# Transposing q and k by the DMA crossbar in place of TensorE, from the third batch on

## The chip, the cores and the metric

The kernel runs on one core of one Trainium2 chip. The metric is the device time of one execution in microseconds. Times are quoted as medians of several runs. A run counts as slow when it lies over 1.5% above the fastest of its kernel. Small differences can still be clear of noise, so 95% intervals are given.

## The reference, cut to what matters

A windowed attention with eight global tokens is followed by a two-layer network with a snake activation. Everything is bf16 inside the kernel.

```python
B, H, S, D = 8, 8, 576, 64              # q, k, v: float32 [B, H, S, D]
mask = (abs(i - j) <= 32) | is_global[i] | is_global[j]
attn = softmax(where(mask, q @ k.T / sqrt(D), -1e9))
x = (attn @ v).transpose(0, 2, 1, 3).reshape(B * S, H * D)      # [4608, 512]
h = x @ w_in                                                    # w_in [512, 2048]
g = h + sin(alpha * h) ** 2 / (alpha + 1e-9)
out = g @ w_out                                                 # w_out [2048, 512]
```

## The kernel before

The work goes in nine rounds. Round p has an attention stage for batch p (the ninth has none), whose gaps are filled with the second-layer matmuls of chunk p-1 (a chunk is 512 tokens), and then a first-layer stage for chunk p (16 blocks of four matmuls). q and k of batch p+1 are loaded in round p's attention stage, and the first two of its four head pairs are transposed inside round p's first-layer stage.

This kernel's scores matmul reads q and k with the head dimension on partitions, so both are transposed. TensorE does it through PSUM, six transposes for k and six for q of each head pair. VectorE spreads k into twelve overlapping key blocks, and ScalarE copies q.

```python
def stage_T(b, hp, qpool, qtag):
    QS, KS = qk[b]                                   # [96, 6, 8 heads, 64]
    for jt in range(NTW):                            # 6
        nc.tensor.transpose(out=Kps[:, WIN + jt * TW : WIN + (jt + 1) * TW],
                            in_=KS[:, jt, 2 * hp : 2 * hp + 2, :], ...)
    nc.vector.tensor_copy(out=kTw[hp][:, :, 0:KB], in_=...)       # from PSUM, 12 windows of 112
    Qps = qpool.tile([P, S], BF, name=qtag)
    for jt in range(NTW):
        nc.tensor.transpose(out=Qps[...], in_=QS[:, jt, 2 * hp : 2 * hp + 2, :], ...)
    nc.scalar.copy(out=qT[hp][:, :, 0:QB], in_=Qps[...])
# ... cut ...
def mm1(c, H2b, psB, sq):                            # first layer, 16 blocks
    for nt in range(NT):
        # four matmuls into one of six PSUM tiles h2
        # ScalarE: Sb = sin(alpha * h2)
        # S2 = Sb * Sb: ScalarE for block 5, VectorE for 10 and 15, POOL for the others
        # VectorE, two blocks later: H2b = S2 / alpha + h2   (frees h2)
# ... cut ...
# in the first-layer stage of round p, batch p+1:
i_ = (10, 13)
m1[i_[0]] = partial(chain, m1[i_[0]], partial(shift_v, p + 1), partial(global_v, p + 1),
                    partial(stage_T, p + 1, 0, psB, "hb"))
m1[i_[1]] = partial(chain, m1[i_[1]], partial(stage_T, p + 1, 1, psB, "hb"))
```

`shift_v` and `global_v` are three transfers on SyncE's queue. They prepare the v of batch p+1. The output stores are on that queue too. In all the timelines below, what the program put on SyncE's queue starts in the order of the program.

The softmax here doesn't subtract the row's maximum and nothing guards it: scores larger than these inputs give would overflow.

## Time and profile before

| | before |
|---|---|
| time, median | 385.99 us (385.66 to 386.37) |
| span of the profiled run | 385.0 us |
| five periods, first-layer stage of round 2 to that of round 7 | 38.5, 38.3, 38.0, 38.4, 38.0 us |

A period is the time from the first first-layer matmul of one round to that of the next. In the profile PE is TensorE and PEld its weight loads, DVE is VectorE, ACT ScalarE, POOL GpSimd and SP SyncE; a q behind a name is that engine's queue of instructions. The granted clock is the share of its full speed at which TensorE was allowed to run. First, from the page of the kernel before, the busy time of each engine, and the engines' shares of the chain of work that ended last:

```profile
PE 336.2 (87%) x3208; PEld 162.9 (42%) x3208; DVE 244.9 (64%) x551; ACT 258.4 (67%) x435; POOL 249.3 (65%) x394
...
PE 52%; ACT 18%; DVE 10%; issue 7%; POOL 7%; DMA 3%; POOLq 1%; ACTq 0%; DVEq 0%
```

Then two periods of it, by windows. The columns are the stretch, its length, busy time and count of PE, PEld, DVE, ACT and POOL, the granted clock, the share of the DMA engines, and GB/s.

```profile
167.28:205.63 38.35, 37.21 (x385) 18.04 (x384) 27.13 (x59) 29.59 (x50) 31.19 (x48) 1.00 0.93 97
205.63:243.60 37.97, 37.15 (x385) 18.05 (x384) 26.63 (x59) 29.58 (x50) 31.28 (x48) 1.00 0.94 98
```

TensorE is busy for nearly the whole period at full clock. The timeline of TensorE in one first-layer stage shows what the transposes take (start, duration, line, operation, tiles, shape, count, and in brackets the idle time before it and what ended it):

```profile
205.63 9.66 PE L457 MATMUL hb<-xT,w_in 128*128 128x512 bf16 x44
215.13 0.42 PE L304 MATMUL Kps<-identb,KS 96*128 96x96 bf16 x6
215.39 0.42 PE L319 MATMUL hb<-identb,QS 96*128 96x96 bf16 x6
215.64 2.76 PE L457 MATMUL hb<-xT,w_in 128*128 128x512 bf16 x12
218.87 0.42 PE L304 MATMUL Kps<-identb,KS 96*128 96x96 bf16 x6 [0.47 <-DVE kTw L310]
...
221.25 1.89 PE L494 MATMUL ops<-w_out,H2b 128*128 128x512 bf16 x8
```

The starts are 0.26 us apart, so six transposes take TensorE 0.26 us, and the eight groups of a batch take 2.1 us. The same stretch on VectorE:

```profile
216.11 1.28 DVE L472 TENSOR_TENSOR S<-Sb 128x512 bf16<-128x512 bf16 x1 [0.22 <-ACT Sb L464]
217.31 0.73 DVE L447 SCALAR_TENSOR_TENSOR H2b<-S,recipT,hb 128x512 bf16<-128x512 bf16 x1
217.97 0.84 DVE L310 COPY kTw<-Kps 128x1344 bf16<-128x1344 bf16 x1
218.74 2.05 DVE L447 SCALAR_TENSOR_TENSOR H2b<-S,recipT,hb 128x512 bf16<-128x512 bf16 x3
...
222.22 0.44 DVE L472 TENSOR_TENSOR S<-Sb 128x512 bf16<-128x512 bf16 x1
```

The same square takes 1.28 us while POOL squares beside it and 0.44 us after. In these 6.5 us VectorE works without a pause. SyncE's queue in this stage:

```profile
206.55 0.33 SPq L506 DMA_DIRECT2D out_dram<-osb  x1
207.18 0.51 SPq L121 DMA_DIRECT2D VW<-VW  x1
207.74 0.58 SPq L122 DMA_DIRECT2D VW<-VW  x1
208.37 0.78 SPq L127 DMA_DIRECT2D VW<-VgN  x1
```

### The profile page before, as it was taken

To read this page: it belongs to the slowest core of one execution; us is meant where nothing else is said; L and a number is where in the kernel's file an instruction comes from. 1 tells how busy PE (TensorE), PEld (TensorE's weight loads), DVE (VectorE), ACT (ScalarE), POOL (GpSimd) and SP (SyncE) were. 2 spreads that over 40 slices of the span, in tenths; PEclk is the share of its full clock that TensorE was granted. 3 is DMA by queue.
4 is the path that set the end of the run, shared out by engine and by line. 5 is a ranking of instruction groups with operands and counts; after the bars stand their busy time and mean duration, and the time that the engine had idled before them with its cause. 6 is when DMAs were issued, how large, how long until landed. Compare 5 with 4: busy or idle time off the path is not lost.

```text
span 385.0 us, 8609 instructions
## 1 busy us (share of the span) xinstructions
PE 336.2 (87%) x3208; PEld 162.9 (42%) x3208; DVE 244.9 (64%) x551; ACT 258.4 (67%) x435; POOL 249.3 (65%) x394
## 2 busy tenths in 40 slices
PE   1128499798999999999999999999999999999796
PEld 0015244443444444444544444444444444344342
DVE  7725459574977497649774976497749774954500
ACT  1057487786988588858885888578857885744310
POOL 8934396227878589858986898689768006854400
PEclk9999999999999999999999999999999999999989
DMA  6999999257999409940994099409940001000012
GB/s 53 136 162 161 190 164 165 37 77 77 155 132 153 124 9 103 148 127 7 103 148 126 7 103 149 128 6 113 137 128 5 30 30 54 2 28 27 29 54 82
DMA packets 133723, 35.31 MB, mean 92 GB/s; under 512 B 123314, under 2 KB 128178, under 8 KB 133682
## 3 DMA queue, kind: packets, MB, share of 16 engines
q0 software_dynamic: 122560, 19.02, 69.4%
q1 hardware_dynamic: 8034, 15.54, 13.9%
q10 hardware_dynamic: 3088, 0.21, 0.8%
q8 instruction: 25, 0.41, 0.4%
q14 instruction: 16, 0.13, 0.1%
HBM read 38.42 MB, written 9.44 MB: 124 GB/s over the span
## 4 chain that ended last, share of the span: by engine, by line
PE 52%; ACT 18%; DVE 10%; issue 7%; POOL 7%; DMA 3%; POOLq 1%; ACTq 0%; DVEq 0%
PE hb L457 22%; PE ops L494 13%; PE o L494 8%; ACT Sb L464 6%; ACT E L342 4%; DMA KS<-in_k_dram 3%; DVE H2b L447 3%; PE num L375 3%; ACT S L470 2%; DVE S L472 2%; DVE kTw L310 2%; ACT lnd L358 2%; PE hb L494 2%; ACT rec L360 2%; PE Sp L336 2%
## 5 line engine op out<-in xcount | busy, mean ns | idle before, releaser
L457 PE MATMUL hb<-xT,w_in 128*128 128x512 bf16 x576 | 133.1, 384 | 6.0 <-POOL xT L402 4.8
L464 ACT ACTIVATE Sb<-hb,alphaT 128x512 bf16<-128x512 f32 x144 | 96.6, 684 | 55.2 <-PE hb L457 53.9
L447 DVE SCALAR_TENSOR_TENSOR H2b<-S,recipT,hb 128x512 bf16<-128x512 bf16 x144 | 102.6, 741 | 29.3 <-POOL S L472 28.8
L472 POOL TENSOR_TENSOR S<-Sb 128x512 bf16<-128x512 bf16 x91 | 92.6, 1040 | 34.1 <-ACT Sb L464 31.5
L457 PEld LDWEIGHTS <-w_in 128*128 128x128 bf16 x576 | 56.5, 99 | 74.4 <-issue 10.9
L494 PE MATMUL ops<-w_out,H2b 128*128 128x512 bf16 x320 | 81.7, 385 | 3.2 <-DVE osb L502 3.0
L494 PEld LDWEIGHTS <-H2b 128*128 128x128 bf16 x576 | 50.6, 98 | 58.6 <-issue 7.3
L344 DVE TENSOR_TENSOR E<-E,MASK 128x672 bf16<-128x672 bf16 x64 | 34.1, 534 | 32.9 <-ACT E L342 32.2
L494 PE MATMUL o<-w_out,H2b 128*128 128x512 bf16 x224 | 54.7, 380 | 0.0
L342 ACT ACTIVATE E<-Sp 128x672 bf16<-128x672 f32 x64 | 45.9, 717 | 4.1 <-PE Sp L336 4.0
L402 POOL COPY xT<-xg 128x4 bf16 x64 | 12.9, 201 | 48.9 <-DVE xg L400 45.5
L107 POOL DMA_DIRECT2D VW<-in_v_dram x56 | 42.5, 776 | 0.7 <-issue 0.3
L358 ACT ACTIVATE lnd<-den 128x288 f32<-128x288 f32 x64 | 26.4, 412 | 18.3 <-PE den L352 17.8
L382 DVE TENSOR_TENSOR xT<-num,rec 128x288 bf16<-128x288 f32 x64 | 28.7, 449 | 6.1 <-PE num L375 4.8
L375 PEld LDWEIGHTS <-VW 128*64 128x64 bf16 x768 | 18.3, 116 | 33.1 <-DVE gn L386 10.9
L472 DVE TENSOR_TENSOR S<-Sb 128x512 bf16<-128x512 bf16 x30 | 18.3, 609 | 21.5 <-ACT Sb L464 20.6
L375 PE MATMUL num<-E,VW 128*64 128x56 bf16 x768 | 25.3, 201 | 6.9 <-DVE gn L386 3.1
L360 ACT ACTIVATE rec<-lnd 128x288 f32<-128x288 f32 x64 | 28.3, 443 | 2.0
L310 DVE COPY kTw<-Kps 128x1344 bf16<-128x1344 bf16 x32 | 27.1, 848 | 1.9 <-PE Kps L304 1.9
L336 PE MATMUL Sp<-qT,kTw 64*128 64x56 bf16 x768 | 22.1, 190 | 6.0 <-ACT E L342 4.1
L100 POOL DMA_DIRECT2D QS<-in_q_dram x30 | 23.2, 774 | 3.0 <-DMA QS<-in_q_dram 3.0
L324 ACT COPY qT<-qp 128x576 bf16<-128x576 bf16 x20 | 12.7, 633 | 18.4 <-PE ops L268 13.2
(73 smaller groups left out, 305.1 us busy)
## 6 DMA issues: line engine op xcount, KB each, us to landing
out_dram<-osb SPq DMA_DIRECT2D x36, 256.0 KB
VW<-in_v_dram POOLq DMA_DIRECT2D x40, 112.0 KB, 4.8
VW<-VW SPq DMA_DIRECT2D x8, 384.0 KB
KS<-in_k_dram POOLq DMA_DIRECT2D x30, 96.0 KB, 4.7
QS<-in_q_dram POOLq DMA_DIRECT2D x30, 96.0 KB, 4.7
w_in<-in_moe_w_in_dram POOLq DMA_DIRECT2D x4, 512.0 KB, 8.0
w_out<-in_moe_w_out_dram POOLq DMA_DIRECT2D x4, 512.0 KB, 13.1
VW<-VW SPq DMA_DIRECT2D x8, 240.0 KB
```

Source lines behind the costliest of these rows:

```text
L107: nc.gpsimd.dma_start(out=W[p0 : p0 + n, par, u, :].rearrange("p (h d) -> p h d", d=D), in_=v[b, :, key0 : key0 + n, :].rearrange("h p d - ...
L310: nc.vector.tensor_copy(out=kTw[hp][:, :, 0:KB], in_=bass.AP(tensor=base.tensor, offset=base.offset, ap=[list(base.ap[0]), [QB, NW], [1, KB]],
L342: nc.scalar.activation(out=E[:], in_=Sp[:, :, 0:EW], func=AF.Exp, scale=scale)
L344: nc.vector.tensor_tensor(out=E[:], in0=E[:], in1=mk[:, None, :].to_broadcast([P, 2, EW]), op=ALU.mult)
L358: nc.scalar.activation(out=lnd[:], in_=den[:, :, 0:QB], func=AF.Ln)
L360: nc.scalar.activation(out=rec[:], in_=lnd[:], func=AF.Exp, scale=-1.0)
L375: nc.tensor.matmul(out=num[pr, u, :], lhsT=W[:, i % 2, i // 2, c0 : c0 + 64], rhs=E[:, t, u * QC : (u + 1) * QC], start=True, stop=True, s ...
L447: nc.vector.scalar_tensor_tensor(out=H2b[:, n_, :], in0=s_[:], scalar=recipT[:, n_ : n_ + 1], in1=h_, op0=ALU.mult, op1=ALU.add,)
L457: nc.tensor.matmul(out=h2[:], lhsT=w_in[:, ci, nt * P : (nt + 1) * P], rhs=xT[:, ci, c * CH : (c + 1) * CH], start=(ci == 0), stop=(ci == ...
L464: nc.scalar.activation(out=Sb[:], in_=h2[:], func=AF.Sin, scale=alphaT[:, nt : nt + 1])
L472: eng.tensor_tensor(out=S2[:], in0=Sb[:], in1=Sb[:], op=ALU.mult)
L494: nc.tensor.matmul(out=ops[:], lhsT=H2b[:, nt, ts * P : (ts + 1) * P], rhs=w_out[:, nt, :], start=(nt == 0), stop=(nt == NT - 1),)
```

## The change

The intent is to take the transposes off the busiest engine. From batch 2 on (the third), SyncE issues twelve crossbar transposes per batch from SBUF to SBUF. (A crossbar transpose is a transfer that transposes what it moves; the profile calls it DMA_TRANSPOSE.) VectorE copies k and q from there, so for these batches the PSUM bank, the ScalarE copies and the TensorE transposes are not used.

```diff
+    kTn = const.tile([P, NHP, KSP], BF, name="kTn")
+    qTn = const.tile([P, NHP, S], BF, name="qTn")
+    def turn(b):
+        for jt in range(NTW):
+            for src, dst, c0 in ((KS, kTn, WIN), (QS, qTn, 0)):
+                fs.append(partial(nc.sync.dma_start_transpose,
+                    out=dst[:, :, c0 + jt * TW : c0 + (jt + 1) * TW],
+                    in_=src[:, jt].rearrange("p h d -> p (h d)")))
+    def stage_W(hp):
+        nc.vector.tensor_copy(out=kTw[hp][:, :, 0:KB], in_=...)      # 12 windows, from kTn
+        nc.vector.tensor_copy(out=qT[hp][:, :, 0:QB], in_=qTn[:, hp].rearrange(...))
 # ... cut: head pairs 2 and 3 in the attention stage, the loads of batch 2 by tile ...
             if 1 <= p and p + 1 < B:
-                i_ = (10, 13)
-                m1[i_[0]] = partial(chain, m1[i_[0]], partial(shift_v, p + 1), partial(global_v, p + 1), partial(stage_T, p + 1, 0, psB, "hb"))
-                m1[i_[1]] = partial(chain, m1[i_[1]], partial(stage_T, p + 1, 1, psB, "hb"))
+                tf = turn(p + 1)
+                i_ = (10, 13) if p > 1 else (12, 14)
+                with_extra(m1, tf, 1 if p > 1 else 4, 2)
+                m1[i_[0]] = partial(chain, m1[i_[0]], partial(shift_v, p + 1), partial(global_v, p + 1), partial(stage_W, 0))
+                m1[i_[1]] = partial(chain, m1[i_[1]], partial(stage_W, 1))
```

Each transpose turns 96 tokens of all eight heads. So the copies of the first head pair need all twelve.

More of the change, by code (lines that the diff above doesn't have):

```diff
@@ L201 @@
         zero(kTw[hp][:, :, KB:P])
+    zero(kTn[:, :, 0:WIN])
+    zero(kTn[:, :, WIN + S : KSP])
     zero_v(1)
@@ L326, in stage_T @@
         )
+    def turn(b):
+        QS, KS = qk[b]
+        fs = []
+        for jt in range(NTW):
+            for src, dst, c0 in ((KS, kTn, WIN), (QS, qTn, 0)):
+                fs.append(partial(
+                    nc.sync.dma_start_transpose,
+                    out=dst[:, :, c0 + jt * TW : c0 + (jt + 1) * TW],
+                    in_=src[:, jt].rearrange("p h d -> p (h d)"),
+                ))
+        return fs
+    def stage_W(hp):
+        base = kTn[:, hp, 0:1]
+        nc.vector.tensor_copy(
+            out=kTw[hp][:, :, 0:KB],
+            in_=bass.AP(
+                tensor=base.tensor, offset=base.offset,
+                ap=[list(base.ap[0]), [QB, NW], [1, KB]],
+            ),
+        )
+        nc.vector.tensor_copy(
+            out=qT[hp][:, :, 0:QB], in_=qTn[:, hp].rearrange("p (i c) -> p i c", c=QB)
+        )
     EW = NU * QC
@@ L433, in attention @@
         for hp, j in t_at.items():
-            parts[j + LEAD] = partial(chain, parts[j + LEAD], partial(stage_T, b, hp, psA, "qp"))
+            t_ = partial(stage_T, b, hp, psA, "qp") if b < 2 else partial(stage_W, hp + 2)
+            parts[j + LEAD] = partial(chain, parts[j + LEAD], t_)
         return parts, partial(stage_G, b, gn, gr)
@@ L574 @@
                 else:
-                    for tag, shape, dt_ in (
-                        ("num", [P, NU, QC], F32), ("den", [P, NU, QC], F32),
-                        ("qp", [P, S], BF), ("o2", [P, DM], F32),
-                    ):
-                        psA.tile(shape, dt_, name=tag)
+                    if p == 1:
+                        for tag, shape, dt_ in (
+                            ("num", [P, NU, QC], F32), ("den", [P, NU, QC], F32),
+                            ("qp", [P, S], BF), ("o2", [P, DM], F32),
+                        ):
+                            psA.tile(shape, dt_, name=tag)
                     fill = mm2(p - 1, H2[p - 1], ((psC, "ops"), (psA, "o2")) * 2)
-                    parts, last = attention(p, psA, {2: -1, 3: 1})
+                    parts, last = attention(p, psA, {2: -1, 3: 1} if p == 1 else {0: -1, 1: 1})
                     counts = [1] * NP_
@@ L597 @@
                     if p + 1 < B:
-                        ld = load_slots(p + 1, p == 1)
+                        ld = load_slots(p + 1, False)
                         if p == 1:
```

## The prediction

> **What bounds the kernel now.** From 129 to 320 us the kernel repeats a period of about 38.2 us (the stages by windows: 38.4, 38.4, 38.0, 38.4, 38.0): one first-layer stage (16 blocks) and one attention stage filled with second-layer matmuls. In it TensorE is busy 37.2 us, POOL 31.2, ScalarE 29.6, VectorE 26.6-27.3, at full granted clock. The chain of waits is mostly TensorE. But in the first-layer stage (205.6 to 221.4 us) POOL squares nearly back to back (13 x 1.04 us), and VectorE works without a pause from about 216 to 225 us; the timeline shows fourth-block second-layer matmuls starting at 224.56, right when VectorE's last H2b ends. So TensorE is first, with POOL and VectorE close behind.
>
> **What goes.** Per batch, 48 transposes; the timeline shows each group of six taking 0.26 us of TensorE, so 8 x 0.26 = 2.1 us, plus 0.47 us waiting for the single Kps bank and about 0.3 us in attention: 2.5 us. Also four ScalarE copies of 0.63 us and four VectorE copies of 0.85 us from PSUM. Six batches (2 to 7): at most 15 us (4%).
>
> **What comes.** (a) Twelve crossbar transposes of 96x512 per batch on SyncE's queue. No such transfer is in this trace. SyncE's plain issues take 0.5 to 0.8 us, and the DMA engines are almost idle in this stage (windows, 251-260 us). They start after the previous output store (206.5 us); the first copy wants all twelve by about 217 us, so each may take some 0.7-0.8 us[...]. [...]each 0.1 us per transpose costs about 1 us a period. (b) Eight VectorE copies SBUF to SBUF. My estimate is 0.4-0.5 us for the key block and 0.2-0.3 for q, if VectorE goes at twice the rate of the PSUM copy. [...]VectorE's square of nt 10 takes 1.28 us beside POOL, 0.44 without. The copies in slots 10 and 13 run while POOL squares, so I expect each to take up to 1 us more, and POOL to lose about 1.2 us a period.
>
> **On the critical path.** The 2.5 us leave TensorE's stream, but the first-layer stage then comes to POOL's chain (13.1 us plus a gap) and VectorE's H2b chain, delayed by the blocked copies. I expect 1.5-2.5 us of new TensorE waits per period, mostly before first-layer block 15, the first scores and the fourth second-layer group. Net about -0.3 us x 6.
>
> **Prediction:** 384 us, 372 to 402. Faster by over 2%: 0.30; within: 0.42; slower: 0.28.
>
> **What shows it.** TensorE busy falls by about 13 us; period 37.9 us. The copies of slots 10 and 13 last much longer than those in attention. If landing were late, VectorE's first key-block copy would wait for a DMA, by the list of waits, and TensorE would idle several us at block 15. If neither, the period is near 35.7 us.
>
> **What would make it wrong.** Transposes at over 1 us each: 400 us and beyond. Copies without blocking and fast transposes: 372. Batch 2, whose loads are issued in its own first-layer stage, may wait for its late loads in any case.

2.5 us leave, 1.5 to 2.5 come, and the net that I put down was about -0.3 us for each of six batches, so 386 - 2 = 384 us. The 0.7 to 0.8 us are my estimate of what may go to each transpose: the 10.5 us from 206.5 to 217, less an allowance for the landing, over twelve. The 1 us a period for each 0.1 us is that count of twelve. The copies' times are estimates from the 0.85 us of the copy from PSUM; twice its rate was an assumption (measured later: 0.84 us from PSUM, 0.50 from SBUF, which is 1.7 times). That a copy loses up to 1 us is an estimate from the one square (1.28 - 0.44 = 0.84 us); that POOL loses too was not shown.

## The result and the profile after

| | before | after |
|---|---|---|
| time, median | 385.99 us | 428.06 us (426.45 to 429.31) |
| ratio of fast runs, 95% interval | | 1.108 (1.104 to 1.112) |
| mean granted clock of the profiled run | 0.996 | 0.94 |
| period of batch 2's transposes (round 1 to round 2) | 38.1 us | 47.2 us |
| the five periods after it | 38.5, 38.3, 38.0, 38.4, 38.0 | 45.4, 45.3, 44.9, 44.4, 45.4 |

A ratio is the mean time of one kernel's fast runs over that of the other's of the same rounds, so it is not quite the ratio of the medians.

The five periods add 34.2 us and batch 2's adds 9.1. Round 1's first-layer stage starts 0.8 us earlier, which takes that much back. Together this is the 42.5 us by which the spans differ. The same lines of the page as shown of before:

```profile
PE 336.0 (79%) x2920; PEld 153.0 (36%) x2920; DVE 250.3 (59%) x577; ACT 245.9 (58%) x411; POOL 249.7 (58%) x390
...
PE 38%; SPq 17%; DVE 10%; ACT 10%; POOL 9%; issue 7%; DMA 7%; POOLq 1%; DVEq 0%; ACTq 0%
```

TensorE has 288 instructions fewer and yet the same busy time, because its clock is lower (0.92 in the windows below; runs that follow do the same work at 1.00 in about 35 us per period). And 17% of the chain is now SyncE's queue, which was not in it before. Two periods by windows:

```profile
182.57:227.84 45.27, 37.10 (x338) 16.43 (x337) 28.06 (x63) 27.39 (x46) 31.58 (x48) 0.92 0.90 108
227.84:272.76 44.92, 36.81 (x337) 16.30 (x336) 28.32 (x63) 27.49 (x46) 31.71 (x48) 0.92 0.92 109
```

SyncE's queue in the first-layer stage that starts at 272.76 us:

```profile
274.11 1.23 SPq L469 DMA_TRANSPOSE kTn<-KS  x1
275.43 1.20 SPq L469 DMA_TRANSPOSE qTn<-QS  x1
276.72 1.21 SPq L469 DMA_TRANSPOSE kTn<-KS  x1
...
288.69 1.21 SPq L469 DMA_TRANSPOSE qTn<-QS  x1
290.19 0.53 SPq L123 DMA_DIRECT2D VW<-VW  x1
...
291.40 0.78 SPq L129 DMA_DIRECT2D VW<-VgN  x1
```

SyncE is held 1.21 us by each transpose, and they start 1.30 us apart. The transfers of v, which stood at 207 to 209 us before (1.5 us into the stage), now stand behind them, 17.4 us into the stage. VectorE in the same stage:

```profile
283.24 1.28 DVE L502 TENSOR_TENSOR S<-Sb 128x512 bf16<-128x512 bf16 x1 [0.21 <-ACT Sb L494]
284.45 0.73 DVE L477 SCALAR_TENSOR_TENSOR H2b<-S,recipT,hb 128x512 bf16<-128x512 bf16 x1
289.90 0.51 DVE L346 COPY kTw<-kTn 128x1344 bf16<-128x1344 bf16 x1 [4.72 <-DMA kTn<-KS]
291.22 0.31 DVE L353 COPY qT<-qTn 128x576 bf16<-128x576 bf16 x1 [0.81 <-DMA qTn<-QS]
291.45 2.06 DVE L477 SCALAR_TENSOR_TENSOR H2b<-S,recipT,hb 128x512 bf16<-128x512 bf16 x3
293.42 1.31 DVE L346 COPY kTw<-kTn 128x1344 bf16<-128x1344 bf16 x1
```

The copies wait 5.5 us for the landing, and three H2b operations stand behind them in VectorE's queue. Those free PSUM tiles that TensorE needs:

```profile
272.76 12.25 PE L487 MATMUL hb<-xT,w_in 128*128 128x512 bf16 x56
285.23 1.02 PE L487 MATMUL hb<-xT,w_in 128*128 128x512 bf16 x4 [0.22 <-DVE H2b L477]
292.24 1.87 PE L487 MATMUL hb<-xT,w_in 128*128 128x512 bf16 x4 [5.99 <-DVE H2b L477]
```

TensorE stops before block 15 for 6.0 us. The four matmuls after the stop take 1.87 us in place of 1.02: the granted clock is 0.50 from 288.2 to 295.1 us, and 1.00 in the 2 us before and in the 2 us behind that. It falls during the stop and stays low for 2.8 us behind it, which makes the loss larger.

### The profile page after: what moved, and what is told of

The parts are those of the page before. It is cut to its first block, busy times and chain, and to the rows that moved or that the text cites. A ratio compares the mean times of both kernels' runs of the same rounds, so it can differ in the third digit from the quotient of the medians.

```text
span 427.5 us, 8203 instructions
## 1 busy us (share of the span) xinstructions
PE 336.0 (79%) x2920; PEld 153.0 (36%) x2920; DVE 250.3 (59%) x577; ACT 245.9 (58%) x411; POOL 249.7 (58%) x390
## 4 chain that ended last, share of the span: by engine, by line
PE 38%; SPq 17%; DVE 10%; ACT 10%; POOL 9%; issue 7%; DMA 7%; POOLq 1%; DVEq 0%; ACTq 0%
SPq L469 16%; PE ops L524 16%; PE hb L487 9%; PE o L524 5%; PE num L404 3%; DMA qTn<-QS 3%; ACT E L371 2%; DVE H2b L477 2%; DMA VW<-VgN 2%; ACT Sb L494 2%; POOL VW L109 2%; DMA VW<-in_v_dram 2%; DVE qT L353 2%; DVE E L373 2%; PE hb L524 2%
## 5 line engine op out<-in xcount | busy, mean ns | idle before, releaser
L487 PE MATMUL hb<-xT,w_in 128*128 128x512 bf16 x576 | 136.0, 390 | 37.4 <-DVE H2b L477 32.5
L524 PE MATMUL ops<-w_out,H2b 128*128 128x512 bf16 x320 | 89.5, 413 | 3.2 <-DVE osb L532 3.0
L524 PEld LDWEIGHTS <-H2b 128*128 128x128 bf16 x576 | 52.3, 102 | 65.8 <-issue 18.2
L373 DVE TENSOR_TENSOR E<-E,MASK 128x672 bf16<-128x672 bf16 x64 | 32.4, 507 | 33.8 <-ACT E L371 33.8
L109 POOL DMA_DIRECT2D VW<-in_v_dram x56 | 43.8, 791 | 5.9 <-PE Sp L365 4.9
L346 DVE COPY kTw<-kTn 128x1344 bf16<-128x1344 bf16 x24 | 16.8, 700 | 31.9 <-DMA kTn<-KS 27.5
L404 PEld LDWEIGHTS <-VW 128*64 128x64 bf16 x768 | 18.4, 116 | 38.9 <-DVE gn L415 13.8
L102 POOL DMA_DIRECT2D KS<-in_k_dram x36 | 28.1, 781 | 4.6 <-DVE kTw L296 2.5
L102 POOL DMA_DIRECT2D QS<-in_q_dram x36 | 28.0, 778 | 2.7 <-DMA VW<-in_v_dram 1.5
```

The lines of the kernel that those rows point to most:

```text
L102: nc.gpsimd.dma_start(out=dst[:, t, :, :], in_=src[b, :, t * TW : (t + 1) * TW, :].rearrange("h p d -> p h d"),)
L109: nc.gpsimd.dma_start(out=W[p0 : p0 + n, par, u, :].rearrange("p (h d) -> p h d", d=D), in_=v[b, :, key0 : key0 + n, :].rearrange("h p d - ...
L373: nc.vector.tensor_tensor(out=E[:], in0=E[:], in1=mk[:, None, :].to_broadcast([P, 2, EW]), op=ALU.mult)
L404: nc.tensor.matmul(out=num[pr, u, :], lhsT=W[:, i % 2, i // 2, c0 : c0 + 64], rhs=E[:, t, u * QC : (u + 1) * QC], start=True, stop=True, s ...
L487: nc.tensor.matmul(out=h2[:], lhsT=w_in[:, ci, nt * P : (nt + 1) * P], rhs=xT[:, ci, c * CH : (c + 1) * CH], start=(ci == 0), stop=(ci == ...
L524: nc.tensor.matmul(out=ops[:], lhsT=H2b[:, nt, ts * P : (ts + 1) * P], rhs=w_out[:, nt, :], start=(nt == 0), stop=(nt == NT - 1),)
```

## The experiments

Theory A: SyncE issues a transpose every 1.30 us, so the twelfth lands 11 x 1.30 + 2.3 = 16.6 us after the first starts (2.3 us is what the last one took from its start to its landing), and VectorE's queue carries the wait on to TensorE. Rival B: crossbar traffic itself slows other transfers or engines. Rival C: the copies are slow beside POOL's work and load VectorE.

### The transposes without a reader

The kernel before, plus the transposes of batches 3 to 7, written to buffers that nothing reads.

```diff
                 i_ = (10, 13)
+                if p > 1:
+                    with_extra(m1, turn(p + 1), 1, 2)
```

> The kernel before, plus the twelve crossbar transposes of the change for batches 3 to 7, written to buffers that nothing reads. Theory A (SyncE issues a transpose every 1.30 us, so the twelve land 15.6 + 2.4 us after the first, and the VectorE copy that waits for them holds up the first-layer stage): nobody waits, so 386 to 390 us, at most a little more because the shift of v stands behind them in SyncE's queue. Rival B (crossbar traffic slows other transfers or engines by itself): 410 us or more.

It took 415.4 us, ratio 1.073 (1.066 to 1.080). (Its profile fell in a slow run of 420.6 us.) So theory A as stated fell: nobody waits for these transposes, and most of the loss is there. (The expectation names what stands behind them, but as "at most a little more".) The trace names a second victim, in TensorE's timeline:

```profile
204.98 0.59 PE L389 MATMUL num<-E,VW 128*64 128x56 bf16 x12 [6.76 <-DMA VW<-VgN]
249.64 0.60 PE L389 MATMUL num<-E,VW 128*64 128x56 bf16 x12 [5.61 <-DMA VW<-VgN]
```

The first values matmul waits for v, whose three transfers were issued behind the transposes. In the kernel after, this wait is hidden behind the other one. It had to be told from rival B, which predicts the same time. Not all of the wait is lateness. In the periods that start in rounds 2 to 5 it is 5.5 to 7.1 us, and ends 8.1 to 10.0 us after the last of the three was issued. In the one that starts in round 6, which has no loads for a next batch, it is 2.5 us, and ends 5.4 us after. So the late transfers of v probably also met those loads and took longer. (All this is read from the one profile, of the slow run.)

### The copies without the wait

The change, but from batch 3 on the transposes land in a dump, and the copies read batch 2's q and k. The values are wrong. The run still counted as correct, because scores of this size make the attention nearly uniform and the tolerance is wide; computed off the chip, the error of batches 3 to 7 is 0.015 in place of 0.004.

```diff
-            for src, dst, c0 in ((KS, kTn, WIN), (QS, qTn, 0)):
+        ks, qs = ((KS, kTn, WIN), (QS, qTn, 0)) if b == 2 else ((KS, dump, 0), (QS, dump, 0))
# ... cut: the six transposes of k now come ahead of the six of q ...
```

> The change, but from batch 3 on the transposes land in a buffer that nothing reads, and the VectorE copies read batch 2's transposed q and k (wrong result on purpose). All transposes and all copies are still there, only the wait is gone. Theory A: the five later periods of 45.1 us fall to 37 to 38.5, the stage of batch 2 keeps its 9 us, so 388 to 396 us. Rival B (traffic) or rival C[...]: 410 us or more.

It took 424.1 us, ratio 1.099 (1.094 to 1.103), with periods of 42.0 to 44.5 us: a miss again. TensorE waits 2.5 to 4.1 us per period for v here, and 2.5 us around the end of the first-layer stage for H2b, delayed by the copies. Taking away the first wait lets the second one show.

### Transposes issued earlier

The transposes of batches 3 to 7 go into the attention stage before, two behind each of its last six steps.

```diff
                             with_extra(parts, ld, 0, 4)
+                            with_extra(parts, turn(p + 1), 5, 2)
# ... cut: batch 2's stay in the first-layer stage ...
```

> The change, but from batch 3 on the transposes are issued during the attention stage before, two behind each of its last six steps, as soon as their loads have landed. Right result. Theory A: they land before the first copy wants them, periods of 37 to 38.5 us, 386 to 396 us in all (batch 2 still waits). Rival B: contention with the loads of q, k and v, 405 us or more. Rival C: as after, over 410.

It took 400.3 us, ratio 1.037 (1.032 to 1.042), with periods of 39.5 to 40.0 us up to round 6. The copies no longer wait for a landing, and neither does v. This is 28 us off the kernel after. It is above the range that I had written, as the periods stay 1.3 us above those before; batch 2's, where the wait was expected, is 46.8 us.

### Transposes by head pair

Eight transposes of 96x768 in place of twelve of 96x512, in the order in which the copies want them, with the loads by head. (Sizes are also counted in tiles, here 16x128 elements: 36 in place of 24.) Batch 2's start at block 9 in place of 4.

```diff
-        QS = qkp.tile([TW, NTW, H, D], BF, name="QS")
+        QS = qkp.tile([TW, NHP, NTW, 2, D], BF, name="QS")
-        for jt in range(NTW):
+        for hp in range(NHP):
...
+                    in_=src[:, hp].rearrange("p t h d -> p (t h d)"),
```

> Eight transposes per batch in place of twelve, one for q and one for k of each pair of heads (96 x 768 each), pair by pair, with loads by head. Right result. If a transpose costs by its size, each takes 1.8 to 2.0 us of issue, the eight about as long as the twelve (15 us), but the first copy needs only two: Theory A: no wait of VectorE above 1 us in periods 3 to 7, and 385 to 396 us. If the cost is by the instruction, each takes 1.3 us. Rival B or C: over 405 us.

It took 404.0 us, ratio 1.047 (1.039 to 1.055), with periods of 39.3 to 39.4 us up to round 6, and 38.5 in the last; batch 2's was 49.3. SyncE's queue, two of its transposes:

```profile
141.53 1.28 SPq L469 DMA_TRANSPOSE kTn<-KS  x1
142.92 1.20 SPq L469 DMA_TRANSPOSE qTn<-QS  x1
144.22 1.22 SPq L469 DMA_TRANSPOSE kTn<-KS  x1
```

They start about 1.3 us apart (142.92 to 144.22; the median of the run is 1.32), the same for 36 tiles as for 24 (1.30), so up to this size the cost goes by the instruction. In bytes this is 96 x 512 x 2 per 1.30 us = 76 GB/s, and 96 x 768 x 2 per 1.32 us = 112 GB/s. VectorE waits for no landing in rounds 3 to 7 any more. This agrees with theory A for the periods: fewer transposes ahead of the first copy, and 5.9 us of the period are gone (45.1 us mean after, 39.2 here). I missed the total, because batch 2's stage was no better (a values matmul waits 9.8 us for v, which stood behind transposes that waited 9.9 us for the loads of k) and because the waits for H2b, 1.3 and 0.9 us per period, stayed.

### Is it the traffic, or the order in the queue?

Theory D, formed on the first run: the transposes hurt the transfers of v only because these stand behind them in SyncE's queue. To test it, the kernel with unread transposes issues the transfers of v first. Rival B expects no gain from that, since the traffic is the same.

```diff
+                m1[0] = partial(chain, m1[0], partial(shift_v, p + 1), partial(global_v, p + 1))
                 if p > 1:
                     with_extra(m1, turn(p + 1), 1, 2)
-                m1[i_[0]] = partial(chain, m1[i_[0]], partial(shift_v, p + 1), partial(global_v, p + 1), partial(stage_T, p + 1, 0, psB, "hb"))
+                m1[i_[0]] = partial(chain, m1[i_[0]], partial(stage_T, p + 1, 0, psB, "hb"))
```

> The kernel with the unread transposes of before (which took 415 us), but the three transfers that shift v and spread its global rows are issued ahead of the transposes in SyncE's queue. Theory D (a transpose holds SyncE's queue for 1.3 us, so the transfers behind it come 15 us late and the first values matmul waits for v): the waits of 5.5 to 7.1 us per period for v go away, 386 to 390 us. Rival B (crossbar traffic itself costs time): still above 405 us.

The result was wrong (relative error 0.245). I had moved batch 2's transfers too, and its v is loaded late, so at block 0 the loads had not been issued yet. It took 394.95 us, ratio 1.021 (1.018 to 1.025). Its five later periods were already 38.0, 38.9, 38.0, 38.0 and 38.0 us, but a kernel with a wrong result is poor evidence, so I mended it.

```diff
+                sv = 0 if p > 1 else 10
-                m1[0] = partial(chain, m1[0], partial(shift_v, p + 1), partial(global_v, p + 1))
+                m1[sv] = partial(chain, m1[sv], partial(shift_v, p + 1), partial(global_v, p + 1))
```

> The kernel before with unread transposes and v's transfers ahead of them, mended: batch 2's v is shifted where it was (the run of this before gave a wrong result, as its shift read batch 2's v too early, and had a 5.7 us wait in that stage). Theory D: 385 to 388 us, periods of 38.0 us, within 1% of the kernel before. If crossbar traffic has a cost of its own, 390 us or more.

It is correct and took 387.16 us, ratio 1.0006 (0.995 to 1.006), with periods of 38.0 to 38.4 us. SyncE's queue of it:

```profile
168.72 0.52 SPq L123 DMA_DIRECT2D VW<-VW  x1
169.29 0.58 SPq L124 DMA_DIRECT2D VW<-VW  x1
169.92 0.78 SPq L129 DMA_DIRECT2D VW<-VgN  x1
170.74 2.22 SPq L453 DMA_TRANSPOSE kTn<-KS  x1
```

The same sixty transposes that cost 7% ahead of v's transfers cost nothing that shows behind them (0.6% at most, by the interval). Rival B falls: with v first, the crossbar's traffic slows nothing that TensorE waits for. What set off the loss of the unread transposes was order in one queue; as said above, meeting the loads probably made the late v later still.

### What do the copies cost?

With v first, the kernel with stale copies has no wait for SyncE left. What remains is the cost of the copies and the gain on TensorE. (Again the values of batches 3 to 7 are wrong.)

```diff
+                if p > 1:
+                    m1[0] = partial(chain, m1[0], partial(shift_v, p + 1), partial(global_v, p + 1))
```

> The kernel with transposes to a dump and copies of batch 2's data (424 us), with v's transfers ahead of the transposes. Wrong result on purpose. Theory D: the wait of 3 to 4 us per period for v goes, and what is left is the copies alone: periods of 39.4 us as in the early and by-head kernels, 400 to 406 us in all with batch 2's stage (9 to 11 us). Rival B: still above 415 us.

It took 404.3 us, ratio 1.045 (1.040 to 1.049). Batch 2's period is 49.5 us, the five later ones 39.1, 39.5, 39.9, 39.2 and 38.6, a mean of 39.3 against 38.2 before. So the change would lose 1 us per period even with transposes that nobody waits for. VectorE shows why:

```profile
192.72 0.73 DVE L348 COPY kTw<-kTn 128x1344 bf16<-128x1344 bf16 x1
193.37 1.14 DVE L355 COPY qT<-qTn 128x576 bf16<-128x576 bf16 x1
...
196.41 1.31 DVE L348 COPY kTw<-kTn 128x1344 bf16<-128x1344 bf16 x1
197.64 0.59 DVE L355 COPY qT<-qTn 128x576 bf16<-128x576 bf16 x1
```

The four copies take 3.8 us, and TensorE waits 0.22 + 1.35 + 0.96 us for H2b. TensorE waits a further 0.72 and 0.64 us before two values matmuls, for VectorE's small sums; before the change such waits came to 0.5 us per period. Theory E: it is their place that is dear, as POOL squares beside them. So the same copies were moved to the head of the first-layer stage, where POOL has no squares yet:

```diff
-                i_ = (10, 13) if p > 1 else (12, 14)
+                i_ = (0, 0) if p > 1 else (12, 14)
```

> As the run before it in this list, but the copies of the first two head pairs stand at the head of the first-layer stage, where POOL has no squares yet, in place of slots 10 and 13. Wrong result on purpose. Theory E (beside POOL's squares the copies are blocked and cost 3.7 us of VectorE in place of 1.6): they take 0.51 and 0.31 us there, TensorE's waits of about 2.5 us per period at the end of the first-layer stage shrink to under 1 us, the period falls from 39.4 to 36.0-37.5 us, so 10 to 17 us less than that run. If the copies cost by their length alone, the period stays within 0.5 us.

It took 388.6 us, ratio 1.006 (1.001 to 1.010), with periods of 36.6, 36.6, 36.6, 36.7 and 36.2 us (batch 2's still 49.4). VectorE:

```profile
177.29 0.50 DVE L348 COPY kTw<-kTn 128x1344 bf16<-128x1344 bf16 x1
177.70 0.30 DVE L355 COPY qT<-qTn 128x576 bf16<-128x576 bf16 x1
177.92 0.50 DVE L348 COPY kTw<-kTn 128x1344 bf16<-128x1344 bf16 x1
178.34 0.30 DVE L355 COPY qT<-qTn 128x576 bf16<-128x576 bf16 x1
```

The four take 1.6 us, and of the waits for H2b 0.22 us is left. Theory E holds as far as the place goes: one line of placement is worth 2.7 us per period. The copies themselves are shorter by 2.2 us there. But the move also takes them out of the way of the H2b operations, and how much of the 2.7 us is POOL and how much is this was not told apart. With transposes and copies out of the way, the change's own gain is 38.2 - 36.5 = 1.7 us per period.

### Correct kernels that use this

The stale kernels only measure. A correct one needs batch 2 left on TensorE (its loads come too late), v ahead of the transposes, the copies at the head of the stage, and so the first two head pairs transposed in the attention stage before. The first try used four transposes of 96x1536 per batch, to hold SyncE less often. (The expectation calls this 48 tiles; counted as above it is 72.) Its edit is shown against the kernel by head pair.

```diff
-        for hp in range(NHP):
+        for h0 in (0, 2):
-                    in_=src[:, hp].rearrange("p t h d -> p (t h d)"),
+                    in_=src[:, h0 : h0 + 2].rearrange("p a t h d -> p (a t h d)"),
...
+                            if p + 1 > 2:
+                                with_extra(parts, turn(p + 1)[:2], 8, 2)
...
+                    m1[0] = partial(chain, m1[0], partial(stage_W, 0), partial(stage_W, 1))
+                    with_extra(m1, turn(p + 1)[2:], 1, 2)
```

> All of it together, right result: batch 2 as before by TensorE; from batch 3 on four large transposes per batch (96 x 1536 each, loads by head), half of them in the attention stage before; v's transfers ahead of them; copies of the first two head pairs at the head of the first-layer stage. If a transpose costs 1.3 us of SyncE whatever its size (24 and 36 tiles both took 1.3), four cost 5.3 us; if by size beyond that, 48 tiles cost up to 2.5 us each. Expected period 36 to 37.5 us for batches 3 to 7, 374 to 382 us in all, faster than both kernels. If another limit shows, 384 to 390 us.

It is correct and took 386.8 us, ratio 1.003 (0.996 to 1.009): a miss. Batch 2's period is 38.1 us again, as before the change, but the later ones are 37.8 to 39.0. The transposes of 72 tiles hold SyncE for 1.4 to 3.5 us (median 2.4, twice the 1.2 of 36 tiles), and the first two stood in the queue behind an output store that waits 8.3 us for its data. So q landed late:

```profile
171.29 1.04 DVE L354 COPY qT<-qTn 128x576 bf16<-128x576 bf16 x1 [2.74 <-DMA qTn<-QS]
```

The mended version goes back to one head pair per transpose (36 tiles), and issues the first four ahead of that store (shown against the first try):

```diff
-        for h0 in (0, 2):
+        for hp in range(NHP):
...
-                                with_extra(parts, turn(p + 1)[:2], 8, 2)
+                                with_extra(parts, turn(p + 1)[:4], 5, 4)
...
-                    with_extra(m1, turn(p + 1)[2:], 1, 2)
+                    with_extra(m1, turn(p + 1)[4:], 1, 2)
```

> As the large-transpose kernel (386.8 us), but with eight transposes of 36 tiles (1.3 us each), the first four issued before the second output store in SyncE's queue, not after it, so that they land about when the first-layer stage begins; the copies of two head pairs at its head. Right result. The 2.7 us that VectorE waited there for the landing should be under 1 us: periods of 36.6 to 37.5 us for batches 3 to 7, 378 to 383 us in all. If the landing is still late[...], 385 to 390.

It is correct and took 380.7 us, ratio 0.987 (0.982 to 0.993). The periods are 37.2, 36.9, 37.5, 37.1 and 36.2 us. One period by windows:

```profile
164.98:201.92 36.94, 34.47 (x331) 15.94 (x336) 27.41 (x63) 27.39 (x46) 33.55 (x52) 1.00 1.24 131
```

The trace has 331 matmuls here to 336 weight loads, so some matmul records are missing, and the 34.5 us are too low. In the last kernel below, whose trace misses none, TensorE is busy for 35.3 us in place of 37.2, at full clock. It is what the change was meant to do. The transposes are not cheap for SyncE here either: most hold it 1.2 to 1.5 us, some up to 3.2. Yet nothing urgent stands behind them. Waits of about 1.0 and 0.5 to 0.8 us remain ahead of values matmuls in the attention stage.

A rival repair keeps the transposes in the first-layer stage behind v and the k copies in blocks 10 and 13, and gives the q copies to ScalarE, so that VectorE has less to copy beside POOL:

```diff
-        nc.vector.tensor_copy(
+        nc.scalar.copy(
             out=qT[hp][:, :, 0:QB], in_=...
```

> Batch 2 by TensorE, eight transposes in the first-layer stage behind v's transfers, key copies on VectorE in slots 10 and 13 as in the change, but the q copies on ScalarE as in the kernel before. Right result. VectorE loses two of the four blocked copies (0.6 and 1.1 us there), so the period should be about 1.5 us less than the 39.4 us of the by-head kernel: 37.5 to 38.3, and 382 to 387 us in all.

It is correct and took 383.7 us, ratio 0.995 (0.989 to 0.9999), with periods of 37.2, 37.2, 38.0, 37.4 and 37.2 us: it works too, but less well. Last, the better kernel with only the q copies of head pairs 2 and 3 (those in the attention stage) on ScalarE:

```diff
-        nc.vector.tensor_copy(
+        (nc.vector.tensor_copy if hp < 2 else nc.scalar.copy)(
             out=qT[hp][:, :, 0:QB], in_=...
```

> The early-pairs kernel (380.7 us) with the q copies of the last two head pairs, which stand in the attention stage, on ScalarE as in the kernel before. Right result. There TensorE still waits 1.0 and 0.5 to 0.8 us per period for VectorE's small sums, right behind these copies; without 0.6 and 0.3 us of VectorE before them, these should shrink by about 0.5 us in all: periods of 36.6 us for batches 3 to 7, 377 to 380 us in all, at or just past 2% faster than the kernel before. If ScalarE is as late there as VectorE, no change.

It is correct and took 379.96 us (378.6 to 380.7), against 386.15 for the kernel before in the same five rounds, ratio 0.984 (0.980 to 0.988). It beats both kernels, though by less than the 2% at which I would call a kernel faster. Its periods are 36.7, 36.8, 37.6, 36.4 and 36.0 us. The page and one period by windows:

```profile
PE 327.1 (86%) x2968; PEld 153.5 (41%) x2968; DVE 241.7 (64%) x566; ACT 252.0 (67%) x425; POOL 260.8 (69%) x414
166.66:203.41 36.75, 35.29 (x336) 16.09 (x336) 26.29 (x62) 28.22 (x48) 33.44 (x52) 1.00 1.26 133
```

## Why the prediction was wrong

The means of the five later periods, in one sum, which closes by construction since each term is a difference of two runs:

| step | us per period | from |
|---|---|---|
| transposes leave TensorE, copies in a good place | -1.7 | before 38.2, to stale copies at the head 36.5 |
| the same copies at blocks 10 and 13, beside POOL's squares | +2.7 | to stale copies at blocks 10 and 13, v first: 39.3 |
| waits for the transposes and what stands behind them | +5.8 | to the kernel after 45.1 |

By the traces, the 5.8 us are 4.0 us more waiting of TensorE and 1.7 us more busy time, for the same matmuls at the lower clock.

1. **What bounds the kernel: right.** TensorE was first, with VectorE and POOL close behind. The delays of VectorE came through to TensorE, as that says they would.
2. **2.5 us leave TensorE: nearly right.** In traces that miss no matmul, its busy time per period is 35.0 (stale copies at the head) to 35.3 us (the last kernel) in place of 37.2 where the clock is full, so 1.9 to 2.2 us leave, near the 2.1 of the transposes; the 0.47 us wait for the Kps bank goes too. But "TensorE busy falls by about 13 us" did not show in the kernel after (336.2 to 336.0), as its clock is lower there (0.92 in most periods). In the last kernel it falls by 9.1 us, for five batches and not six.
3. **The copies: right in their times, and the waits a little too small.** "0.4-0.5 us for the key block and 0.2-0.3 for q" are 0.50 and 0.30, and beside POOL they go up to 1.31 and 1.14 (by what mechanism was not shown). New TensorE waits of "1.5-2.5 us" are 0.22 + 1.35 + 0.96 = 2.5 in the run that has only them (stale copies at blocks 10 and 13, v first), which with the 2.5 us that leave would make a net of zero, near my -0.3. The measured net is +1.0. The traces of the five periods account for it: on average 1.7 us of busy time and 0.5 of wait for Kps leave, and 2.4 us of waits for H2b and 0.7 more before values matmuls come. The last I did not see. (The best repaired kernel gains 1.6 us per period.) POOL's loss ("about 1.2 us a period", my estimate) was smaller: its busy time per period went from 31.2 us to 31.6.
4. **The step that failed: "each may take some 0.7-0.8 us".** This term was mis-sized. The landing, for which I had made an allowance without a trace to go by, takes 2.3 us, but a transpose takes SyncE 1.30 us from start to start. I had taken the 0.5 to 0.8 us of plain issues, and had derived 0.7 to 0.8 as what would be fast enough, not as what it would be. The estimate that I wrote beside it, about 1 us per period for each 0.1 us per transpose, gives 5.5 us for the 0.55 over, near the 5.7 that issuing earlier and the 5.9 that issuing by head pair took away, and the 5.8 of the table. That it comes so near is partly luck, as 1.7 of the 5.8 is the lower clock, which the estimate knows nothing of. I had also written "Transposes at over 1 us each: 400 us and beyond". The trace before held no such transfer, so it showed neither time; I put into the forecast the figure of another operation.
5. **What I did not see: the transfers of v behind the transposes.** In the kernel after they start 17.4 us into the stage in place of 1.5. Alone this costs 7% (the unread transposes, with the loads that v then meets), and in the kernel after it hides behind the wait of the copies: that was what kept the first two experiments from showing a gain.
6. **Batch 2: named, but not in the sum.** Its period grew by 9.1 us, two more per cent of the time. With its transposes on TensorE the period is 38.1 us again. Which part of it is late loads and which is the rest of its stage was not told apart.

Open as well: why the granted clock falls during a stop of TensorE and stays low behind it, why transposes of 72 tiles, and some smaller ones beside other transfers, hold SyncE up to 3.5 us, and how much a late v loses to the loads that it meets.

## What to carry to other kernels

Do not count a transfer as free because its engine idles: multiply the time that one issue holds its queue by the number of issues (here 12 x 1.30 = 15.6 us), and look at what stands behind them in order. An operation with no duration in the trace deserves a range that also holds a pessimistic figure; here 0.5 to 0.8 us of plain issues stood for a transpose of 1.30. Look for a place where a copy within SBUF on VectorE has neither POOL's work beside it nor urgent work behind it; here, the same four copies took 1.6 us in such a place and 3.8 beside POOL's squares, and the move was worth 2.7 us per period, more than the 2.5 us that the change was to take off TensorE. And compare the counts of matmuls and weight loads before you read a busy time: in one trace here, lost records hid 0.8 us of a period.
